# Converting v on GpSimd: one product per head with a number per partition, in place of one product of two tensors per block

## The chip, the cores and the metric

The kernel runs on one core of a Trainium2 chip. The metric is the device time of one execution in microseconds (us), lower is better. Engines: TensorE (PE; its weight loads are PEld), VectorE (DVE), ScalarE (ACT), GpSimd (POOL) and SyncE (SP, which here only issues DMAs). On-chip memory is SBUF, with 128 partitions; matmul results land in PSUM.

## What is computed

Attention with a decay by a forget gate, followed by a two-layer block with a gate (SiLU) over all tokens. Cut to what matters:

```python
batch, n_heads, seq, head_dim = (8, 8, 576, 64)
scores = scale * np.matmul(q, k.transpose(0, 1, 3, 2))
cum = np.cumsum(np.log(np.clip(f, 0.0001, 1.0)), axis=-1)
decay = cum[:, :, :, None] - cum[:, :, None, :]
scores = np.where(causal, -1000000000.0, scores + decay)
attn = softmax(scores)
x = (attn @ v) as 4608 tokens x 512
h = x @ w_in                       # 512 -> 2048
out = (h * sigmoid(h)) @ w_out     # 2048 -> 512
```

The decay factors: exp(cum_q - cum_k). The factor of the query cancels in the softmax, and the factor of the key is a weight w per key and head. The kernel therefore multiplies each row of v, and a column of ones beside it that gives the sum of the softmax, by w of that key and head.

## The kernel before

The 64 (batch, head) pairs are handled as 32 units of two heads: unit n is batch n // 4 and p = n % 4, with heads p and p + 4. The keys and queries of a sequence are cut into a first block of 128 rows, three more of 128 (`NR` = 3), and a tail of 64 (`ST`). The first blocks of all batches are done early. Then a loop over m = 0 to 15 takes two units a round; a round has a fixed order of instructions for every engine, written out by hand, in which pieces of the two matrix products of the second layer are placed between the steps of attention by a small planner (`fill`, `slot`, `rest`, `ones`). Every engine works through its own list in that order; nothing is reordered at run time.

The steps that the change and the prediction speak of:

- `load_v(b, c)` (L190): SP's queue loads rows 128 + 128c and on of v of batch b, all eight heads, as float32 into `vf`, 128 partitions x 8 heads x 65 (the last column holds ones). There are four such tiles, one for each c. The fourth block, c = 3, is the tail of 64 rows, in partitions 64 to 127.
- `convert_v(b, c)` (L429): GpSimd multiplies the block by the weights `w_bf` and writes bf16 into `vp`, of which there are two, for even and odd batches. A block of c = 0, 1, 2 is one instruction over 128 partitions x 520 elements, the weights read as a tensor repeated along the 65 columns. The tail is two instructions over 64 partitions x 260: heads 0 to 3 go to partitions 64 to 127 of the output, heads 4 to 7 to partitions 0 to 63.
- `turn(n)` is called once per unit. On GpSimd it puts, in this order: the casts of unit n + 3 to bf16 (`cast_qk`, L409 and L413, which wait for q's load), the issue of the two k transfers of unit n + 4 (`load_qk`, L160), and, in `prepare`, where p is 2 or 3, the conversion of blocks 0 and 1 (p = 2) or 2 and 3 (p = 3) of the next batch. On SP it puts the q loads of unit n + 4 (L169), v's loads of the next batch where p = 1, the tails' loads where p = 2 (L179), and then the transpose of unit n + 3 by DMA (`transposes`, L443), which waits for the casts.
- `scores(n, c)` (L475 on TensorE, L480 and L486 on ScalarE): scores of unit n and their exponentials, into `u` and, for the tail's queries, `ut`.
- `mask(n)` (L492) and `mask_tail(n)` (L498): VectorE multiplies the exponentials of the diagonal blocks by a triangle of ones, `u` x `tri` and `ut` x `trit`. Both inputs lie in SBUF.
- `attend(n)`: TensorE multiplies the exponentials by the converted v (L522; the tail's queries L531) into `dn`; VectorE takes the reciprocal of the sum (L539) and scales the result into `xr` (L540).
- `m1_chunk`: TensorE, `hp` = x times a block of w_in (L583); ScalarE, `th` = tanh of half of it (L591); VectorE, `gt` = (th + 1) x `hp` (L592), which frees `hp`. Its four PSUM buffers (tag "big") are shared with `dn`, `po` and others.
- `m2_part` (L628) and `m2_rows` (L654): `gt` times w_out, into `po` or `pr`; then a copy to SBUF and the store, issued by SP (L607).

In a round with `m2_rows`, which is nearly every one from m = 0 on, the order around the conversion is: scores of unit n, turn(n), one half of `m2_rows`, mask(n), more scores, turn(n + 1), the other half, mask_tail(n), mask(n + 1), scores, attend(n), mask_tail(n + 1), pieces of the second layer, attend(n + 1), more pieces. So p = 2 and p = 3 are the two units of an odd m, and the next batch's v is read from the following round on.

Of the kernel before, what the change touches and what calls it, by code (L numbers as in the profile page):

```python
# [9 lines left out]
ALU = mybir.AluOpType  # L10
FP32 = mybir.dt.float32
BF16 = mybir.dt.bfloat16
P = 128
# [5 lines left out]
def kernel(  # L19
# [10 lines left out]
    nc = tc.nc  # L30

    B, H, S, D = q.shape
    DM, DFF = moe_w_in.shape
    BH = B * H
    NCC = DM // P
    NFC = DFF // P
    NP = H // 2
    SM = 512
    ST = S - SM
    NM = SM // P  # L40
    NR = NM - 1
# [14 lines left out]
    const = ctx.enter_context(tc.tile_pool(name="const", bufs=1))  # L56
# [14 lines left out]
    w_in_bf = const.tile([P, NCC, DFF], BF16, name="w_in_bf")  # L71
    w_out_bf = const.tile([P, NFC, DM], BF16, name="w_out_bf")
    w_bf = const.tile([P, NM + 1, BH], BF16, name="w_bf")
    ident_bf = const.tile([P, P], BF16, name="ident_bf")
    sel = const.tile([P, 2, D], BF16, name="sel")
    ident_f = const.tile([BH, BH], FP32, name="ident_f")
# [5 lines left out]
    junk = const.tile([1, 16], BF16, name="junk")  # L82
    kT0 = [const.tile([P, NP, P], BF16, name=f"kT0_{b}") for b in range(B)]
    v0 = [const.tile([P, H, D + 1], BF16, name=f"v0_{b}") for b in range(B)]
    vps = [const.tile([P, NM, H, D + 1], BF16, name=f"vp_{i}") for i in range(2)]
    uts = [const.tile([P, NM + 1, 3, ST], BF16, name=f"ut_{i}") for i in range(4)]
    vfs = [const.tile([P, H, D + 1], FP32, name=f"vf_{i}") for i in range(4)]

# [63 lines left out]
    def head(p, i):  # L152
        return p + NP * i
# [77 lines left out]
    for i in range(2):  # L231
        nc.vector.tensor_copy(
            out=sel[:, i, :].rearrange("p (a r) -> p a r", a=NP),
            in_=ident_bf[:, :].rearrange("p (r i a) -> p i a r", i=2, a=NP)[:, i, :, :],
        )

    def keep_warm(n):
# [7 lines left out]
        out=f_sb[:, :], in0=f_sb[:, :], scalar1=1e-4, scalar2=1.0, op0=ALU.max, op1=ALU.min  # L245
# [172 lines left out]
    def convert_v(b, c):  # L418
        vbf[b] = vps[b % 2]
        if c < NR:  # L420
            parts = [(slice(0, P), slice(0, P), slice(0, H), slice(0, H))]
        else:
            parts = [
                (slice((1 - i) * ST, (2 - i) * ST), slice(ST, P), slice(0, NP), slice(i * NP, (i + 1) * NP))
                for i in range(2)
            ]
        for ro, r, ho, h in parts:
            w = w_bf[r, c + 1, b * H + h.start : b * H + h.stop, None]
            nc.gpsimd.tensor_tensor(  # L429
                out=vbf[b][ro, c, ho, :],  # L430
                in0=vst[b][c][r, h, :],
                in1=w.to_broadcast([r.stop - r.start, h.stop - h.start, D + 1]),
                op=ALU.mult,
            )
# [71 lines left out]
    def attend(n):  # L506
        b, p = divmod(n, NP)
        if p % 2 == 0:
            xqs[n // 2] = xqp.tile([P, NGR, 2, D], BF16, name="xr", tag="xr", bufs=3)
        xq = xqs[n // 2]  # L510
        u, ut = us.pop(n), uts[n % 4]
        dn = pbig.tile([P, NGR, D + 1], FP32, name="dn", tag="big")

        def vals(kb, i):
            h = head(p, i)
            return v0[b][:, h, :] if kb == 0 else vbf[b][:, kb - 1, h, :]

        for i in range(2):
            for c in range(1, NM):
                for kb in range(c + 1):  # L520
                    o = AT[c, kb]
                    nc.tensor.matmul(  # L522
                        dn[:, i * NR + c - 1, :],
                        lhsT=u[:, i, o : o + P],
                        rhs=vals(kb, i),
                        start=(kb == 0),
                        stop=(kb == c),
                    )
        for j in range(2 * NM + 1):
            kb, i = (j % NM, j // NM) if j < 2 * NM else (NM, 0)  # L530
            nc.tensor.matmul(  # L531
                dn[:, NGR - 1, :],
                lhsT=ut[:, kb, i : i + 2, :].rearrange("p i t -> p (i t)"),
                rhs=vals(kb, i) if kb < NM else vbf[b][:, NR, p, :],
                start=(j == 0),
                stop=(j == 2 * NM),
            )
        rec = recp.tile([P, NGR], FP32, name="rec", tag="rec")
        nc.vector.reciprocal(out=rec[:, :], in_=dn[:, :, D])  # L539
        nc.vector.tensor_tensor(  # L540
            out=xq[:, :, p % 2, :],
            in0=dn[:, :, 0:D],
            in1=rec[:, :, None].to_broadcast([P, NGR, D]),
            op=ALU.mult,
        )
# [280 lines left out]
    for i in range(2):  # L826
        r = slice((1 - i) * ST, (2 - i) * ST)
        nc.gpsimd.tensor_copy(out=trit[r, i, :], in_=tri[r, r])
    for t in uts:
        nc.gpsimd.memset(t[:, 0:NM, 1, :], 0.0)  # L830
    load_w_out(0)
# [62 lines left out]
    for c in range(NM):  # L894
        convert_v(0, c)
# [11 lines left out]
    def prepare(n):  # L907

        b, p = divmod(n, NP)
        if n != NP - 1 and n + 4 < NU:  # L910
            load_qk(n + 4)
        if b + 1 == B:
            return
        if p == 2 and b + 2 < B:
            load_tails(b + 2)
        if b == 0 and p >= 2 or b > 0 and p == 1:
            for c in range(NM) if b > 0 else range(2 * (p - 2), 2 * (p - 1)):
                load_v(b + 1, c)
        if n == NP - 1:
            load_qk(n + 4)  # L920
        if p >= 2:
            for c in range(2 * (p - 2), 2 * (p - 1)) if b > 0 else range(NM * (p - 2)):
                convert_v(b + 1, c)
# [56 lines left out]
    for m in range(NQ):  # L980
# [19 lines left out]
        if m > 0:  # L1000
            if m % 2 == 0:
                b = m // 2 - 1
                pending.append([1 if m == 2 else 2, [REST_OF[b]] + ([TAILS_OF[b][0]] if b == NM - 1 else [])])
        if rows:
# [12 lines left out]
            m2_out(*rows)  # L1017
            passed()
            attend(n)
            mask_tail(n + 1)  # L1020
            if late:
# [3 lines left out]
            else:  # L1025
                slot(1.9, 3)
            attend(n + 1)
            if m < 4:
                if m < 3:
# [18 lines left out]
        mask_tail(n + 1)  # L1048
        slot(piece, 0, (1, 0))
        attend(n)  # L1050
        attend(n + 1)
        slot(min(3.5, max(0.8, behind() - LAG)) if m > 1 else 0.8)
# [40 lines left out]
```

## Time and profile before

| | us |
|---|---|
| median of 3 runs | 339.35 |
| lowest, highest | 338.65, 339.97 |
| the profiled execution, its own time | 341.14 |
| its span, first to last instruction | 339.4 |

Mean granted TensorE clock of the profiled execution: 0.999 of full speed.

| engine | busy us | share of the span | instructions |
|---|---|---|---|
| TensorE | 326.7 | 96% | 4268 |
| TensorE's weight loads | 229.2 | 68% | 4292 |
| ScalarE | 217.2 | 64% | 385 |
| VectorE | 200.5 | 59% | 435 |
| GpSimd | 139.5 | 41% | 223 |

The profile is of one execution; times count from the first instruction. In its lists of groups a row reads: line, engine, operation, output<-inputs with their shapes, count | busy us, mean ns of one | idle us of the engine before them, and what ended that. In a timeline a row reads: start, duration, engine, line, operation, output<-inputs, count of merged instructions, and in brackets how long the engine was idle before and what released it. Neighbours of one kind are merged into one row. An instruction's duration can overlap the next one's start a little.

### The profile page before, as it was taken

Reading aid. Unit: us, or ns where it says so; the run is one execution under the profiler, and the core shown is the slowest. Engines: PE = TensorE matmul, PEld = TensorE weight load, DVE = VectorE, ACT = ScalarE, POOL = GpSimd, SP = SyncE. Lnnn points to the kernel's source line nnn. Section 1 sums busy time; section 2 is a strip of 40 time slices with the busy share of each in tenths; the row PEclk is TensorE's granted clock in tenths of the full one; section 3 lists DMA queues with packets and bytes.
Section 4 is the critical chain, followed back from the end, with each engine's and each line's share of the span. In section 5 each row is a group of like instructions: output and inputs, shape, how many; then the busy total and the mean of one; then the engine's idle time right before and its main releaser. Section 6 shows DMA issues by size and latency. Waiting matters only on the chain.

```text
span 339.4 us, 10334 instructions
## 1 busy us (share of the span) xinstructions
PE 326.7 (96%) x4268; PEld 229.2 (68%) x4292; DVE 200.5 (59%) x435; ACT 217.2 (64%) x385; POOL 139.5 (41%) x223
## 2 busy tenths in 40 slices
PE   7999999999999999999999997999999999999995
PEld 3745566798786767758857894867676676555654
DVE  4668745369568467565656965886673557344330
ACT  5767546687777577758748792866776486344431
POOL 8894426574764664464474352628060000000000
PEclk9999999999999999999999999999999999999999
DMA  8999999999999998997999789959973110001012
GB/s 155 187 189 220 180 215 164 241 171 172 182 188 170 168 186 158 194 190 150 181 179 165 147 148 147 156 115 188 151 108 87 53 38 33 34 33 59 34 62 63
DMA packets 144703, 48.01 MB, mean 141 GB/s; under 512 B 133328, under 2 KB 139728, under 8 KB 144656
## 3 DMA queue, kind: packets, MB, share of 16 engines
q1 hardware_dynamic: 115088, 36.60, 56.9%
q0 software_dynamic: 29408, 10.62, 27.0%
q8 instruction: 33, 0.54, 0.7%
q10 hardware_dynamic: 160, 0.13, 0.2%
q14 instruction: 14, 0.11, 0.1%
HBM read 36.85 MB, written 9.44 MB: 136 GB/s over the span
## 4 chain that ended last, share of the span: by engine, by line
PE 85%; DMA 6%; DVE 4%; POOL 2%; issue 1%; ACT 1%; SPq 1%; POOLq 0%
PE hp L583 33%; PE po L628 20%; PE pr L654 15%; PE sc L475 6%; PE dn L522 5%; DMA vf<-in_v_dram 3%; PE dn L531 2%; DMA qkb<-in_k_dram 1%; PE tp L293 1%; DVE gt L592 1%; DMA qf<-in_q_dram 1%; DVE ut L498 1%; DVE u L343 1%; SPq L443 1%; POOL vp L429 1%
## 5 line engine op out<-in xcount | busy, mean ns | idle before, releaser
L591 ACT ACTIVATE th<-hp 128x384 bf16<-128x384 f32 (+2 forms) x208 | 96.5, 468 | 75.0 <-PE hp L583 68.8
L592 DVE SCALAR_TENSOR_TENSOR gt<-th,hp 128x384 bf16<-128x384 bf16 (+2 forms) x208 | 107.5, 523 | 54.3 <-ACT th L591 44.3
L583 PE MATMUL hp<-x,w_in_bf 128*128 128x384 bf16 (+2 forms) x701 | 120.6, 321 | 0.7 <-DVE gt L592 0.4
L583 PEld LDWEIGHTS <-w_in_bf 128*128 128x128 bf16 x832 | 79.0, 98 | 50.2 <-issue 3.7
L486 ACT ACTIVATE u<-sc 128x1024 bf16<-128x1024 f32 (+1 forms) x96 | 74.3, 811 | 6.9 <-PE sc L475 6.9
L628 PE MATMUL po<-w_out_bf,gt 128*128 128x512 bf16 (+1 forms) x316 | 74.1, 368 | 1.4 <-DVE gt L592 0.2
L654 PE MATMUL pr<-w_out_bf,gt 64*128 64x256 bf16 x1024 | 61.4, 269 | 0.0
L409 POOL CAST qkb<-qf 128x384 bf16<-128x384 f32 x32 | 17.3, 542 | 88.9 <-DMA qf<-in_q_dram 88.3
L654 PEld LDWEIGHTS <-gt 64*128 64x128 bf16 x1024 | 51.2, 94 | 3.9
L628 PEld LDWEIGHTS <-gt 128*128 128x128 bf16 x336 | 32.2, 98 | 27.4 <-issue 0.3
L160 POOL DMA_DIRECT2D qkb<-in_k_dram x56 | 43.9, 786 | 0.8 <-issue 0.7
L429 POOL TENSOR_TENSOR vp<-vf,w_bf 128x520 bf16<-128x520 f32 (+1 forms) x40 | 36.5, 915 | 14.0 <-DMA vf<-in_v_dram 11.9
L638 ACT ACTIVATE osb<-po 128x512 f32<-128x512 f32 (+1 forms) x21 | 12.1, 577 | 26.5 <-PE po L628 26.5
L475 PE MATMUL sc<-qkT 64*128 64x128 bf16 (+1 forms) x640 | 28.2, 206 | 0.4 <-DMA qkT<-qkb 0.3
L492 DVE TENSOR_TENSOR u<-u,tri 128x768 bf16<-128x768 bf16 x32 | 20.2, 631 | 13.5 <-ACT u L486 13.5
L475 PEld LDWEIGHTS <-qkT 64*128 64x128 bf16 x640 | 20.3, 94 | 7.6 <-issue 4.7
L480 ACT ACTIVATE ut<-sc 128x640 bf16<-128x640 f32 x32 | 22.4, 701 | 3.0 <-PE sc L475 2.5
L522 PEld LDWEIGHTS <-u 128*128 128x128 bf16 x576 | 20.6, 97 | 3.1
L522 PE MATMUL dn<-vp,u 128*128 128x65 bf16 x384 | 21.8, 193 | 0.0
L540 DVE TENSOR_TENSOR xr<-dn,rec 128x448 bf16<-128x448 f32 x32 | 20.0, 625 | 1.1
L522 PE MATMUL dn<-v,u 128*128 128x65 bf16 x192 | 20.0, 194 | 0.0
L665 DVE COPY fence<-pr 128x1 f32<-128x1 f32 x16 | 2.5, 158 | 28.0 <-PE pr L654 28.0
(70 smaller groups left out, 243.4 us busy)
## 6 DMA issues: line engine op xcount, KB each, us to landing
out_dram<-osb SPq DMA_DIRECT2D x32, 256.0 KB, 2.9
vf<-in_v_dram SPq DMA_DIRECT2D x26, 256.0 KB, 5.1
qf<-in_q_dram SPq DMA_DIRECT2D x64, 96.0 KB, 3.3
qkb<-in_k_dram POOLq DMA_DIRECT2D x56, 48.0 KB, 4.0
w_in_bf<-in_moe_w_in_dram POOLq DMA_DIRECT2D x4, 512.0 KB, 6.8
w_out_bf<-in_moe_w_out_dram POOLq DMA_DIRECT2D x4, 512.0 KB, 9.1
vf<-in_v_dram POOLq DMA_DIRECT2D x6, 256.0 KB, 9.6
qkb<-in_q_dram POOLq DMA_DIRECT2D x8, 128.0 KB, 4.9
```

Of the source, the lines that this page charges most:

```text
L160: nc.gpsimd.dma_start(out=t2[:, NR + 1 : NX, j * D : (j + 1) * D], in_=k[b, head(p, j), P:SM, :].rearrange("(c p) d -> p c d", p=P),)
L429: nc.gpsimd.tensor_tensor(out=vbf[b][ro, c, ho, :], in0=vst[b][c][r, h, :], in1=w.to_broadcast([r.stop - r.start, h.stop - h.start, D + 1] ...
L475: nc.tensor.matmul(sc[:, i, o : o + q1 - q0], lhsT=kt, rhs=t[r, q0:q1], start=True, stop=True)
L480: nc.scalar.activation(out=ut[:, :, 0:3:2, :].rearrange("p k i t -> p i k t"), in_=sc[:, :, T0 : T0 + (NM + 1) * ST].rearrange("p i (k t) ...
L486: nc.scalar.activation(out=u[:, :, c * SM : c * SM + w], in_=sc[:, :, 0:w], func=ACT.Exp, scale=scale)
L492: nc.vector.tensor_tensor(out=x, in0=x, in1=tri[:, None, None, :].to_broadcast([P, 2, NR, P]), op=ALU.mult)
L522: nc.tensor.matmul(dn[:, i * NR + c - 1, :], lhsT=u[:, i, o : o + P], rhs=vals(kb, i), start=(kb == 0), stop=(kb == c),)
L583: nc.tensor.matmul(hp[:, :], lhsT=w_in_bf[:, cc, fc * P : (fc + 1) * P], rhs=xcols(g, cc), start=(cc == 0), stop=(cc == NCC - 1),)
L591: nc.scalar.activation(out=th[:, :], in_=hp[:, :], func=ACT.Tanh, scale=0.5)
L592: nc.vector.scalar_tensor_tensor(out=gt[:, fc, :], in0=th[:, :], scalar=1.0, in1=hp[:, :], op0=ALU.add, op1=ALU.mult,)
L628: nc.tensor.matmul(po[:, :], lhsT=gt[:, fc, tb * P : (tb + 1) * P], rhs=w_out_bf[:, fc, m0:m1], start=(fc == 0), stop=(fc == NFC - 1),)
L654: nc.tensor.matmul(pos[g, tb][y], lhsT=gt[r, fc, tb * P : (tb + 1) * P], rhs=w_out_bf[r, fc, y * DM // 2 : (y + 1) * DM // 2], start=(half ...
```

## The change

A float32 copy `w_f` of the weights is made once on GpSimd, ahead of the loop. For batches two to seven, `convert_v` issues one `tensor_scalar` for each head: 128 partitions x 65 elements (64 x 65 in the tail), multiplied by one number per partition, which is read from `w_f`. Blocks 0 to 2 take eight instructions each and the tail two times four, so that a batch takes 32 in place of 5. Batches 0 and 1 keep the product of two tensors. The tile `vp` is laid out anew: 3 x 8 + 4 head columns in one dimension in place of 4 blocks x 8 heads, and the readers' index follows.

```diff
+    w_f = const.tile([P, NM, BH], FP32, name="w_f")
...
-    vps = [const.tile([P, NM, H, D + 1], BF16, name=f"vp_{i}") for i in range(2)]
+    vps = [const.tile([P, NR * H + NP, D + 1], BF16, name=f"vp_{i}") for i in range(2)]
...
         for ro, r, ho, h in parts:
+            if b > 1:
+                for x in range(h.stop - h.start):
+                    z = b * H + h.start + x
+                    nc.gpsimd.tensor_scalar(
+                        out=vbf[b][ro, c * H + ho.start + x, :],
+                        in0=vst[b][c][r, h.start + x, :],
+                        scalar1=w_f[r, c, z : z + 1],
+                        scalar2=None,
+                        op0=ALU.mult,
+                    )
+                continue
             w = w_bf[r, c + 1, b * H + h.start : b * H + h.stop, None]
             nc.gpsimd.tensor_tensor(
-                out=vbf[b][ro, c, ho, :],
+                out=vbf[b][ro, c * H : c * H + ho.stop, :],
                 in0=vst[b][c][r, h, :],
                 in1=w.to_broadcast([r.stop - r.start, h.stop - h.start, D + 1]),
                 op=ALU.mult,
...
-            return v0[b][:, h, :] if kb == 0 else vbf[b][:, kb - 1, h, :]
+            return v0[b][:, h, :] if kb == 0 else vbf[b][:, (kb - 1) * H + h, :]
...
-                rhs=vals(kb, i) if kb < NM else vbf[b][:, NR, p, :],
+                rhs=vals(kb, i) if kb < NM else vbf[b][:, NR * H + p, :],
...
+    nc.gpsimd.tensor_copy(out=w_f[:, :, :], in_=w_bf[:, 1 : NM + 1, :])
     for t in uts:
         nc.gpsimd.memset(t[:, 0:NM, 1, :], 0.0)
```

## The prediction

> **What bounds the kernel now.** I read the page's busy slices first, then the stretches, then TensorE's, VectorE's and GpSimd's timelines where TensorE has a hole. The slices of TensorE and GpSimd (each digit is a fortieth of the span, 8.5 us):
>
> ```profile
> PE   7999999999999999999999997999999999999995
> POOL 8894426574764664464474352628060000000000
> ```
>
> TensorE is full from the second slice to the last but one, apart from one 7, the slice from 203.6 us. GpSimd has time to spare and ends at 252 us. The stretches give each engine's busy time in 30 us (PE, PEld, DVE, ACT, POOL):
>
> ```profile
> 170.00:200.00 30.00, 29.93 (x400) 22.32 (x402) 20.57 (x46) 21.88 (x43) 14.19 (x22) 1.00 0.93 158
> 200.00:230.00 30.00, 27.71 (x391) 20.28 (x388) 21.62 (x40) 19.63 (x36) 12.48 (x20) 1.00 0.91 145
> 230.00:260.00 30.00, 29.89 (x416) 21.01 (x414) 19.21 (x38) 19.21 (x34) 12.53 (x19) 1.00 0.87 136
> ```
>
> Converting batches two to seven lies between 99 and 251 us. In that time TensorE stands still for 2.3 us near 203, and for under 0.5 us elsewhere. So the most that this change can win is about 2.7 us, 0.8%. TensorE's hole, and what VectorE did at that moment:
>
> ```profile
> 202.00 1.91 PE L583 MATMUL hp<-xt,w_in_bf 128*128 128x256 bf16 x16
> 206.15 0.60 PE L583 MATMUL hp<-xt,w_in_bf 128*128 128x256 bf16 x4 [2.24 <-DVE gt L592]
> ```
>
> ```profile
> 202.99 2.78 DVE L498 TENSOR_TENSOR ut<-ut,trit 128x128 bf16<-128x128 bf16 x1
> 205.69 1.93 DVE L592 SCALAR_TENSOR_TENSOR gt<-th,hp 128x256 bf16<-128x256 bf16 x5
> ```
>
> `mask_tail` (L498) takes 0.226 us in the median of its 32 and here took 2.78. The gate products (L592) queue behind it on VectorE, they empty the `hp` buffers, and TensorE waits 2.24 us for a buffer. GpSimd at that time:
>
> ```profile
> 201.33 0.50 POOL L409 CAST qkb<-qf 128x384 bf16<-128x384 f32 x1 [0.48 <-DMA qf<-in_q_dram]
> 201.78 0.29 POOL L413 CAST qkb<-qktf 128x128 bf16<-128x128 f32 x1
> 202.02 1.56 POOL L160 DMA_DIRECT2D qkb<-in_k_dram  x2
> 203.60 2.08 POOL L429 TENSOR_TENSOR vp<-vf,w_bf 128x520 bf16<-128x520 f32 x2
> ```
>
> The mask ends 0.1 us after the two v products (203.60 + 2.08 = 205.68). The same pair meets at 234.88: the mask takes 2.44 and ends at 237.32, the products at 237.23. There TensorE had `po` products that need nothing of VectorE, so nothing was lost. All told the two masks, which have both inputs in SBUF, are some 9.7 us over their usual lengths (0.55 and 0.22) in the run; the gate products and `xr`, with one input in PSUM, keep theirs. So a mask and a reading GpSimd instruction hold each other up. This holds for other reading instructions too:
>
> ```profile
> 232.63 0.84 DVE L492 TENSOR_TENSOR u<-u,tri 128x768 bf16<-128x768 bf16 x1 [0.96 <-ACT u L486]
> 232.56 0.50 POOL L409 CAST qkb<-qf 128x384 bf16<-128x384 f32 x1 [0.41 <-DMA qf<-in_q_dram]
> 233.01 0.61 POOL L413 CAST qkb<-qktf 128x128 bf16<-128x128 f32 x1
> ```
>
> The mask waits 0.3 us, goes in between the two casts, and the second cast (usually 0.29) waits in turn. The mask waited for one short instruction, not for both.
>
> **The change part by part.** *The price of one new instruction, t.* The trace has no product with a number per partition. The rows next to it:
>
> ```profile
> L429 POOL TENSOR_TENSOR vp<-vf,w_bf 128x520 bf16<-128x520 f32 x24 | 25.3, 1061 | 12.9 <-DMA vf<-in_v_dram 11.9 <-PE hp L583 0.7
> L429 POOL TENSOR_TENSOR vp<-vf,w_bf 64x260 bf16<-64x260 f32 x16 | 11.1, 697 | 1.1
> L828 POOL COPY trit<-tri 64x64 bf16<-64x64 bf16 x2 | 0.5, 234 | 0.1
> ```
>
> From below: the 384-element cast starts 0.45 before the next instruction and the 128-element one 0.24 (starts above), so 0.82 ns an element and 0.135 fixed; 65 elements make 0.19. From above: a product of 260 elements, 0.62 at its shortest. I take 0.24, the copy of 64 elements, nearest in size, and keep 0.19 and 0.62 for the range.
>
> *GpSimd's work.* A full block goes from one product, about 1.02 from start to start, to eight instructions, 8 x 0.24 = 1.92. The last block goes from two of 0.70 to eight, 1.92. A batch goes from 3 x 1.02 + 2 x 0.70 = 4.5 to 32 x 0.24 = 7.7, six batches add 19 us. They come in trains: blocks 0 and 1 in the turn of a batch's third unit (2.08 becomes 3.84), blocks 2 and 3 in the fourth's (2.44 to 2.80 becomes 3.84).
>
> *What stands behind the trains.* No new wait is added; the first instruction of a block waits for its v transfer as before. Behind a train on GpSimd's queue stand the next unit's two casts and its two k transfers; behind the casts, on SP, that unit's transpose, and behind that stores and the next q loads. After a train of blocks 0 and 1 GpSimd sits idle for 4.9 to 9.3 us for q (before the casts at 107.59, 131.67, 157.07, 182.64, 214.97, 245.91), which swallows 1.8. After blocks 2 and 3 the next cast follows at once in five of six places and would be 1.0 to 1.4 us late. Its units are 11, 15, 19 and so on; counting 24 score products to a unit, unit 11's transpose is issued at 115.09 and its first score stands at 127.00, the others have 14 us or more, a transpose lands in 3.8: nothing lost.
>
> *Who reads the v blocks.* Batches 3 to 7 are read 5 us or more after their last product (136.4 against 141.5, later 6.7 and 13). Batch 2 is tight:
>
> ```profile
> 109.88 2.66 POOL L429 TENSOR_TENSOR vp<-vf,w_bf 128x520 bf16<-128x520 f32 x3
> 114.66 0.28 PE L531 MATMUL dn<-vp,ut 128*128 128x65 bf16 x4
> ```
>
> The last tail product, about 114.7, needs heads 0 and 4 of block 3, the thirteenth instruction of the train: 109.88 + 13 x 0.24 = 113.0, plus the two masks that go in between (0.55 and 0.22): 113.8. Nothing at 0.24; TensorE begins to wait at t = (114.7 - 109.88 - 0.77) / 13 = 0.31 us, and then loses 13 x (t - 0.31). I book 0.1 for this.
>
> *The copy of the weights*, once, 256 elements: by the cast's line 0.35, near 22.8 us. GpSimd idles 4.42 for v at 29.75, but two w_out issues (23.81) go 0.35 later, and SP's later loads wait for one of them (until 35.67). The DMA engines are nine tenths busy there and have older transfers queued: between 0 and 0.35, I book 0.1. The smaller v tile and its new index move no time.
>
> *The masks.* Between instructions of 0.24 the mask waits as it did between the casts, 0.3 at most. At 203 the 2.24 us go; next late there would be TensorE's own order, since `gt` would follow its `th` as in the other rounds. The excess elsewhere cost TensorE nothing and wins nothing.
>
> The Trainium skill, SBUF — State Buffer, Who interferes with whom, speaks against more than that: a VectorE instruction with two SBUF inputs and a GpSimd instruction that reads SBUF exclude each other for a whole instruction. The new one still reads SBUF, so by that page the conflict is cut small and not removed; the trace agrees at 232.63 (0.3 us for one cast), and by it the sum is the same.
>
> **Sum.** 341.14 (own time; span 339.4 and 1.7 around it) - 2.24 + 0.1 + 0.1 = 339.1. The median shown, 339.35, is 1.8 below the profiled execution. I assume that the hole at 203 is in the timed runs too, as the order is fixed, and take the difference as the price of profiling: 339.35 - 2.04 = **337.3**.
>
> **Rivals.**
> - *No change that shows.* The collision needs the mask to arrive within some 2.5 us of a train whose start hangs on a q transfer's landing (0.48 of waiting at 201.33). The 1.8 us between the profiled and the timed runs are near the 2.24: if the timed runs miss the collision, nothing can be won, 339.35 + 0.2 = 339.5. The same if t is 0.40: batch 2 gives back 13 x 0.09 = 1.2, and 338.4 remains. About 339.
> - *The instruction is dear (slower).* At t = 0.62 TensorE waits 13 x 0.31 = 4.0 us for batch 2 at 114.7: 339.35 + 4.0 - 2.2 = 341.1, or 343.5 if the stall at 203 isn't in the timed runs; it decides from t = 0.31 and makes the kernel slower by over 0.5% from 0.61, or 0.44 without the stall. For it: nothing shows what fetching the number costs. Against it: all one-input rows of this size are at 0.3 or below.
> - *The train stays closed (slower).* At 203 the mask didn't get in between the two products (the first ended near 204.67), but behind the second. If sixteen short ones in a row leave no opening either, it waits until 203.60 + 3.84 = 207.44 in place of 205.68, and TensorE 1.8 longer; at 234.88 the same makes up to 1.7 more: 341.1 to 342.8, say 342. Against it: at 217.37 the mask got in after 1.07 us, with a train of three of 2.80. The Trainium skill, GPSIMD Engine Reference, Instruction dispatch, says that the eight cores don't hold each other at the end of an instruction; cores out of step would leave no common gap. The trace agrees at 203 (both products were sat out) and not at 217.
> - That the change doesn't do what it says: the counts would tell (192 instructions in place of 30); I give it nothing.
>
> **Chances.** Forecast 0.42 (336.3 to 337.6: the lower end wins all 2.7 and some of the edges), no change 0.30, dear 0.15, closed train 0.13. What a measurement of this kernel can tell from no change is about 0.5%, 1.7 us: faster than 337.65, 0.42; slower than 341.05, 0.28; between, 0.30. The range reaches from 336.3 to 341.4: it leaves out the worse half of the two slower cases and a little below. The forecast's own range is 336.3 to 338.
>
> **What would show it.** Right: no L498 over 0.8 us, no hole over 0.5 us near 203, new GpSimd instructions at 0.19 to 0.30 from start to start, first `dn` of batch 2 unmoved. Dear: t over 0.31 and a TensorE wait on `vp` near 114. Closed: an L498 of 3 us or more beside a train. The forecast is wrong if the timed runs never had the hole, or if later starts of trains make new collisions where TensorE has only gate work.

## The result and the profile after

| | before | after |
|---|---|---|
| median, us | 339.66 (6 runs, the first three among them) | 343.33 (6 runs) |
| lowest, highest | 338.65, 341.44 | 341.23, 346.23 |
| the profiled execution, own time (span) | 341.14 (339.4) | 345.39 (343.6) |

The ratio is 1.012, 95% interval 1.0087 to 1.0154: the change made the kernel slower by 3.7 us. The page of the changed kernel, slices of the span (lines of the kernel file move by 1 to 13; `mask_tail` is now L510, `mask` L504, the new instruction L432, the old products L441):

```profile
PE   8999999999799799999999999999999999999995
POOL 8985416554779959898798797969679100000000
PEclk9999999999999989999999999999999999999999
```

TensorE's 7 near 203 us is gone. There are others in the slices from 86 and from 112 us, and just behind the second the granted clock dips. GpSimd is busy until 267 us. The stretches (busy us of PE, PEld, DVE, ACT and POOL, then the granted clock, the DMA share and GB/s):

```profile
90.00:130.00 40.00, 37.34 (x531) 26.45 (x529) 24.61 (x56) 25.03 (x44) 31.42 (x63) 0.96 1.13 155
...
170.00:200.00 30.00, 29.47 (x430) 21.94 (x430) 18.35 (x42) 21.16 (x37) 25.75 (x52) 1.00 1.16 159
200.00:230.00 30.00, 30.00 (x447) 23.29 (x445) 19.21 (x48) 21.98 (x42) 23.41 (x49) 1.00 0.96 151
230.00:260.00 30.00, 30.00 (x430) 21.77 (x429) 18.99 (x43) 21.65 (x38) 23.56 (x48) 1.00 1.16 156
```

From 200 us on TensorE has no hole at all. The loss lies before, above all between 90 and 130. TensorE's timeline at its largest hole, and GpSimd's in front of it:

```profile
116.02 0.25 PE L543 MATMUL dn<-vp,ut 128*128 128x65 bf16 x3
118.46 0.19 PE L543 MATMUL dn<-vp,ut 128*128 128x65 bf16 x1 [2.19 <-POOL vp L432]
```

```profile
101.81 6.94 POOL L432 TENSOR_SCALAR vp<-vf,w_f 128x65 bf16<-128x65 f32 x16 [1.20 <-DMA vf<-in_v_dram]
109.41 0.51 POOL L410 CAST qkb<-qf 128x384 bf16<-128x384 f32 x1 [0.66 <-DMA qf<-in_q_dram]
...
111.75 8.28 POOL L432 TENSOR_SCALAR vp<-vf,w_f 128x65 bf16<-128x65 f32 x16
120.10 0.51 POOL L410 CAST qkb<-qf 128x384 bf16<-128x384 f32 x1
```

The train of batch 2's blocks 2 and 3 takes 8.28 us, where the old one took 2.66. The tail product of batch 2's first unit waits 2.19 us for its thirteenth instruction. The list of waits for TensorE from 95 to 200 us (total, times, longest) has this and two smaller ones, at 148 us (0.59, batch 3) and 176 us (0.51, batch 4):

```profile
PE dn L543 <- POOL vp L432: 3.3, 3, 2.2
```

What the hole brought with it shows in narrow stretches (columns as above):

```profile
116.20:119.60 3.40, 1.21 (x10) 0.55 (x7) 0.88 (x3) 0.91 (x3) 2.84 (x8) 0.99 0.42 88
119.60:123.00 3.40, 3.40 (x17) 1.48 (x16) 0.09 (x1) 0.00 (x0) 3.33 (x7) 0.50 0.32 45
```

In 3.4 us TensorE was busy for 1.21, and for the next 3.4 us it was granted half its clock. The 3.4 us of work done there would have taken 1.7 at the full clock, so this costs 1.7 us more.

**Where the 4.2 us of the two profiled executions come from.** I line up the first score product of each unit in both (before, after):

| up to unit | before | after | later by | step |
|---|---|---|---|---|
| 4 | 83.43 | 83.46 | 0.03 | |
| 6 | 96.01 | 97.36 | 1.35 | +1.3, at 87 and 91 us, batch 1, not converted in the new way |
| 10 | 124.42 | 129.79 | 5.37 | +4.0, batch 2: wait 2.19, half clock 1.7 |
| 14 | 152.54 | 158.67 | 6.13 | +0.8, batch 3 |
| 18 | 182.00 | 188.79 | 6.79 | +0.7, batch 4 |
| 22 | 213.56 | 217.97 | 4.40 | -2.4, no hole near 203 |
| 31 | 277.09 | 281.39 | 4.29 | -0.1 |

The three waits on v add up to 3.3 us, near the 3.7 between the medians; only one of the six timed executions was profiled, so how the others divide is not shown. The other steps vary from execution to execution. The 1.3 near 90 us were 0.4 in the kernel of e1 below and 1.4 in that of e5, whose programs are alike up to there. The two runs of the changed kernel that show a granted clock of 1.000 took 342.74 and 342.86 us, against 345.39 for the profiled one (0.995); the fastest, 341.23, shows 0.998.

### The profile page after: what moved, and what is told of

Same layout as the page of the kernel before. It is cut to its first block, busy times and chain, and to the rows that moved or that the text cites. A ratio compares the mean times of both kernels' runs of the same rounds, so it can differ in the third digit from the quotient of the medians.

```text
span 343.6 us, 10508 instructions
## 1 busy us (share of the span) xinstructions
PE 332.0 (97%) x4292; PEld 230.3 (67%) x4292; DVE 194.3 (57%) x435; ACT 217.3 (63%) x385; POOL 200.3 (58%) x386
## 4 chain that ended last, share of the span: by engine, by line
PE 66%; DMA 13%; POOL 12%; SPq 3%; DVE 2%; issue 2%; ACT 1%; POOLq 0%
PE hp L595 24%; PE po L640 19%; PE pr L666 10%; DMA qf<-in_q_dram 6%; POOL vp L432 5%; PE sc L487 4%; DMA vf<-in_v_dram 4%; PE dn L534 4%; DMA w_out_bf<-in_moe_w_out_dram 3%; PE dn L543 2%; SPq L455 2%; POOL v L349 1%; PE wm L241 1%; POOL qkb L161 1%; PE tp L294 1%
## 5 line engine op out<-in xcount | busy, mean ns | idle before, releaser
L432 POOL TENSOR_SCALAR vp<-vf,w_f 128x65 bf16<-128x65 f32 (+1 forms) x192 | 88.6, 478 | 5.6 <-DMA vf<-in_v_dram 1.2
L640 PE MATMUL po<-w_out_bf,gt 128*128 128x512 bf16 (+1 forms) x336 | 79.1, 374 | 0.2
L504 DVE TENSOR_TENSOR u<-u,tri 128x768 bf16<-128x768 bf16 x32 | 19.0, 593 | 15.0 <-ACT u L498 15.0
L551 DVE RECIPROCAL rec<-dn 128x7 f32<-128x7 f32 x32 | 6.5, 204 | 22.4 <-PE dn L543 22.4
```

What stands on the lines that cost most here:

```text
L432: nc.gpsimd.tensor_scalar(out=vbf[b][ro, c * H + ho.start + x, :], in0=vst[b][c][r, h.start + x, :], scalar1=w_f[r, c, z : z + 1], scalar2 ...
L640: nc.tensor.matmul(po[:, :], lhsT=gt[:, fc, tb * P : (tb + 1) * P], rhs=w_out_bf[:, fc, m0:m1], start=(fc == 0), stop=(fc == NFC - 1),)
```

## The experiments

My theory after this result ("late v", later "price"): the new instruction costs about 0.43 us, nearly twice what I took, and the loss is batch 2 reaching its reader late, with batches 3 and 4 behind it; the collision with the masks is solved. Rivals: the loss comes from the copy of the weights at the start ("start"); or longer trains cost something in every batch ("load"). All diffs are against the changed kernel.

**e1, the copy and the layout alone.**

```diff
-            if b > 1:
+            if b > B:
```

> The copy of the weights and the new layout of vp stay; all batches are converted by products of two tensors again. Theory 'late v' (the new instruction takes 0.44 us, so batches 2 to 4 are read before they are ready, which costs 2.2, 0.6 and 0.5 us and a spell at half clock; the collision near 203 is gone, which wins 2.2): same time as before, within 0.5 us, and the long mask_tail with its hole of some 2 us is back in odd rounds from 200 us on. Rival 'start' (the 1.3 us that the profiled execution of the changed kernel lost between 84 and 92 us, where batch 1 is read, come from the copy and what it delays): 1 to 1.5 us slower than before.

Ratio to before 1.0003, interval 0.9978 to 1.0027. The rival "start" falls. But the expected hole near 203 wasn't there in the profiled execution, though the products were the old ones: one `mask_tail` took 2.46 us, at 233, and TensorE lost nothing by it. That pointed at the hole itself (e11).

**e2, batches 5 to 7 alone.**

```diff
-            if b > 1:
+            if b > 4:
```

> Per-head instructions for batches 5, 6 and 7 alone. Theory 'late v': these batches had 13 us between their last product and their first reader, trains of 7 to 8 us fit, no wait of TensorE on vp from 100 us on, and the collisions at 203 and 235 are gone: 1 to 2.3 us faster than before (337.4 to 338.7). Rival 'load' (longer trains delay the casts, the k transfers and SP's queue in every batch): half of the loss stays, 341 or more. If the timed runs of before don't have the hole: same as before.

338.89 against 339.26, ratio 0.9974, interval 0.9948 to 0.9999. No wait of TensorE on `vp` past 100 us, so half of the new instructions cost nothing, and "load" falls. The gain, 0.4 us between the medians and 0.9 by the ratio, is below the least expected, and the interval all but reaches 1.

**e3, batches 2 to 4 alone.**

```diff
-            if b > 1:
+            if 1 < b <= 4:
```

> Per-head instructions for batches 2, 3 and 4 alone. Theory 'late v': the waits on vp at about 116, 148 and 176 us stay and the hole near 203 may come back: 2 to 5 us slower than before, at least as slow as the changed kernel. Rival 'load': about half of the loss, 1.5 to 2 us slower than before.

342.36, ratio 1.0098, interval 1.0063 to 1.0133: 3.1 us above before, nearly the whole loss. TensorE's waits in the profile (1.64 at 114 us, 1.64 at 144, 0.50 at 173):

```profile
PE dn L543 <- POOL vp L432: 3.8, 3, 1.6
```

**e4, blocks 0 and 1 of batches 5 to 7.**

```diff
-            if b > 1:
+            if b > 4 and c < 2:
```

> Per-head instructions only for blocks 0 and 1 of batches 5 to 7, the trains that met mask_tail near 203 and 235. Theory 'late v': as the version for whole batches 5 to 7, 1 to 2.3 us faster than before, since the trains of blocks 2 and 3 (near 217 and 249) cost TensorE nothing before. Rival 'load': between that version and before.

338.85, ratio 0.9985, interval 0.996 to 1.001: not told apart from before, where 1 to 2.3 us less was expected.

**e5, e6, e7: the price of one instruction.** In place of the number per partition: the constant 1.0 (e5); a plain copy (e6); a product of two tensors per head (e7). e5 and e6 leave out the weights of batches 2 to 7.

```diff
-                        scalar1=w_f[r, c, z : z + 1],
+                        scalar1=1.0,
```

```diff
-                    nc.gpsimd.tensor_scalar(
+                    nc.gpsimd.tensor_copy(
                         out=vbf[b][ro, c * H + ho.start + x, :],
-                        in0=vst[b][c][r, h.start + x, :],
-                        scalar1=w_f[r, c, z : z + 1],
...
+                        in_=vst[b][c][r, h.start + x, :],
                     )
```

```diff
-                    nc.gpsimd.tensor_scalar(
+                    nc.gpsimd.tensor_tensor(
...
-                        scalar1=w_f[r, c, z : z + 1],
-                        scalar2=None,
-                        op0=ALU.mult,
+                        in1=w_bf[r, c + 1, z : z + 1].to_broadcast([r.stop - r.start, D + 1]),
+                        op=ALU.mult,
                     )
```

> The same instructions with the constant 1.0 in place of the number per partition; leaves out the weights of batches 2 to 7. If fetching the number makes the price: 0.19 to 0.25 us from start to start in place of 0.44. If a scalar instruction of this size costs that whatever the number: 0.4 or more.

> A plain copy with conversion for each head, 65 elements; leaves out the weights of batches 2 to 7. By the casts' line 0.19 us, by the 64-element copy 0.24, from start to start. If cutting into 32 instructions were itself dear: 0.4 or more.

> A product of two tensors for each head, 65 elements. By the line through the 520-element and 260-element products (1.02 and 0.70) it would take 0.46, as dear as the new instruction; if the 260-element ones are dear because they wait for each other, 0.25. Masks: if any short reading instruction lets a mask in, no mask over 0.3 us late.

GpSimd's groups (busy us, mean ns of one) of the changed kernel, and of e5, e6 and e7 in this order:

```profile
L432 POOL TENSOR_SCALAR vp<-vf,w_f 128x65 bf16<-128x65 f32 x144 | 65.4, 476 | 1.6 <-DMA vf<-in_v_dram 1.2
L432 POOL TENSOR_SCALAR vp<-vf,w_f 64x65 bf16<-64x65 f32 x48 | 23.2, 483 | 3.9
```

```profile
L432 POOL TENSOR_SCALAR vp<-vf 128x65 bf16<-128x65 f32 x144 | 50.7, 387 | 1.5 <-DMA vf<-in_v_dram 1.1
```

```profile
L432 POOL CAST vp<-vf 128x65 bf16<-128x65 f32 x144 | 27.8, 242 | 0.2 <-DMA vf<-in_v_dram 0.2
```

```profile
L432 POOL TENSOR_TENSOR vp<-vf,w_bf 128x65 bf16<-128x65 f32 x144 | 38.1, 298 | 0.3
```

An instruction's duration can overlap the next one's start, so I compare medians from start to start (one profiled execution of each), and set beside them how long TensorE waited for batch 2:

| per head, full block | start to start, us | TensorE's wait near 115 us |
|---|---|---|
| copy (e6) | 0.179 | none |
| product of two tensors (e7) | 0.252 | none |
| constant number (e5) | 0.335 | 1.20 |
| number per partition (changed kernel) | 0.422 | 2.19 |

The wait follows the price: thirteen instructions, 13 x (0.422 - 0.335) = 1.13 us more, and the wait grows by 0.99. The constant's 0.335 lies between the two values that I expected. Fetching the number is 0.09 of the price; most of it is the kind of instruction. A product with a second tensor, repeated along the row, is cheaper than a multiplication by one number. In the tail the new instructions stand 0.53 apart: there each begins some 0.08 us after the one before has ended, while in a full block it begins 0.02 before that. Why is not shown; the per-head products stand 0.25 apart in the tail too.

**e8, products of four heads.**

```diff
-                for x in range(h.stop - h.start):
+                n4 = min(4, h.stop - h.start)
+                for x in range(0, h.stop - h.start, n4):
                     z = b * H + h.start + x
-                    nc.gpsimd.tensor_scalar(
-                        out=vbf[b][ro, c * H + ho.start + x, :],
...
+                    nc.gpsimd.tensor_tensor(
+                        out=vbf[b][ro, c * H + ho.start + x : c * H + ho.start + x + n4, :],
...
```

> Blocks 0 to 2 of batches 2 to 7 as two products of four heads, 260 elements, in place of one of eight. Theory 'late v': trains grow by under 1 us, batch 2's last block comes near 113.5, so no wait of TensorE on vp over 0.3 us; what is left is whether a mask gets in between such products: if yes the time is 1 to 2 us below before, if the train stays closed to it, as at 203, equal to before.

339.54 against 339.44, ratio 0.9995, interval 0.9972 to 1.0017. No wait on `vp` past 100 us. The masks next to trains are up to 0.76 us late (984 ns in place of 225), and none of it reaches TensorE. So a mask got in and the time stayed equal, which neither branch of the expectation had.

**e9, a product per head, timed** (the kernel of e7).

> The product of two tensors for each head of batches 2 to 7, as in the single look before (0.25 us from start to start, no wait on vp), now timed. Theory 'price' (what costs is the price of one instruction against batch 2's deadline, not the cutting): not slower than before; 338.2 to 339.3. Rival 'cutting' (32 instructions a batch cost in themselves): 340 or more.

338.85 against 338.90, ratio 0.9997, interval 0.9979 to 1.0016. Cutting a batch's conversion into 32 instructions costs nothing; the kind of instruction does. And it wins nothing either, although these instructions have almost the price, 0.25, that the prediction took.

**e10, batches 3 to 7.**

```diff
-            if b > 1:
+            if b > 2:
```

> The changed kernel with batch 2 converted by products again; batches 3 to 7 per head with a number per partition. Theory 'price': batch 2's wait near 115 us goes, and with it any half-clock spell behind it; batch 3 and 4 may still make TensorE wait, 0.5 to 1.6 us each: 339.5 to 341.5, at least 1.5 us below the changed kernel. If the loss is spread evenly over six batches: 342.5.

339.16 against 338.90, ratio 1.002, interval 0.9994 to 1.0046. This is 0.3 us below the range that I expected. Leaving one batch of six to the old products takes back nearly all: the loss hangs on batch 2. In this kernel TensorE waits nowhere from 95 to 200 us. GpSimd's train of blocks 2 and 3 of batch 2, and the tail product of batch 2's first unit:

```profile
110.95 2.66 POOL L441 TENSOR_TENSOR vp<-vf,w_bf 128x520 bf16<-128x520 f32 x3
```

```profile
115.66 0.28 PE L543 MATMUL dn<-vp,ut 128*128 128x65 bf16 x4
```

Batches 3 and 4 no longer make TensorE wait, so their 0.59 and 0.51 in the changed kernel, and batch 3's 1.64 in e3, needed batch 2's long trains ahead of them.

**e11, the kernel before, once more.** No edit.

> The kernel before, unchanged, profiled once more. If the hole of 2.2 us near 203 us belongs to the fixed order: it is there again. If it belongs to single executions: no hole, and a time near 339.

338.42 us, span 336.6, and no hole. VectorE and GpSimd at the place where the first profile had the mask of 2.78 us:

```profile
202.24 0.62 DVE L540 TENSOR_TENSOR xr<-dn,rec 128x448 bf16<-128x448 f32 x1
202.78 0.22 DVE L498 TENSOR_TENSOR ut<-ut,trit 128x128 bf16<-128x128 bf16 x1
203.07 1.95 DVE L592 SCALAR_TENSOR_TENSOR gt<-th,hp 128x256 bf16<-128x256 bf16 x5
```

```profile
201.68 1.56 POOL L160 DMA_DIRECT2D qkb<-in_k_dram  x2
203.26 2.25 POOL L429 TENSOR_TENSOR vp<-vf,w_bf 128x520 bf16<-128x520 f32 x2
```

Here the mask started 0.48 us ahead of the two products and took its usual 0.22. In the first profile it started 0.61 ahead, even earlier, and was caught. In both it started while GpSimd was issuing k's transfers, and 0.22 us would have ended before the first product. So these starts don't tell the two cases apart, and what held the mask from 202.99 to 203.60 is not shown. Of five profiled executions in which products of two tensors convert batch 5 there (before, e1, e3, e8, e11) one has the hole. Without it there was nothing to win: from the first score product of unit 18 to that of unit 31 TensorE takes 92.6 us in e11, in e2 and in the changed kernel alike, against 95.1 in the first profile.

**e12, one instruction for a whole block, with a constant.** Leaves out the weights of batches 2 to 7.

```diff
-                for x in range(h.stop - h.start):
...
+                nc.gpsimd.tensor_scalar(
+                    out=vbf[b][ro, c * H : c * H + ho.stop, :],
+                    in0=vst[b][c][r, h, :],
+                    scalar1=1.0,
...
```

> One instruction of 520 elements (260 in the tail's halves) with the constant 1.0 in place of eight; leaves out the weights of batches 2 to 7. Against 0.34 us for 65 elements it parts the fixed price from the price of an element: if the fixed part is 0.28, some 0.7 to 0.8 us for 520 elements.

```profile
L430 POOL TENSOR_SCALAR vp<-vf 128x520 bf16<-128x520 f32 x18 | 27.4, 1529 | 2.1 <-DMA vf<-in_v_dram 1.3 <-PE hp L593 0.4
```

1.488 us from start to start, twice what was expected: the price lies in the elements. (1.488 - 0.335) / 455 = 2.5 ns an element and 0.17 fixed, against (1.017 - 0.252) / 455 = 1.7 ns for the product of two tensors.

## Why the prediction failed

- **The step that failed: "I take 0.24, the copy of 64 elements, nearest in size".** The term is the price t; it measured 0.42 in full blocks and 0.53 in the tail. I chose the row by size and not by kind of operation. I worked out 0.8 ns an element from the casts and carried this over to a multiplication by a number; e12 shows three times as much. The trace of before has no row of the right kind on GpSimd: a product of two tensors per head, had it been shown, would have given 0.25 (e7). Only the upper end of the range, 0.62, allowed for what came.
- **Batch 2's deadline: right place, right mechanism.** The thirteenth instruction of that train, the threshold, and nothing at 0.24 are what e7 shows (0.25: no wait). The threshold of 0.31 was too high: at 0.335 it gives 13 x 0.025 = 0.3 us of wait, and e5 had 1.20. In the changed kernel the train began at 111.75, with TensorE 1.35 behind, so 0.5 later against TensorE than before; and the tail's instructions cost 0.11 more than the others, five of them 0.6. The rival "the instruction is dear" gives 13 x (0.42 - 0.31) = 1.4 at the measured price, that is 340.8 to 341 without the gain at 203, so it had the cause and the sign, but less than half of the loss. I had given it 0.15.
- **"I assume that the hole at 203 is in the timed runs too, as the order is fixed": wrong.** e11, e1 and e3 don't have it. The order is fixed, but the start of a train follows a q transfer, and the profile of one execution can't tell a hole of the program from a hole of that execution. The 1.8 us between the profiled execution and the median was largely the hole, not the price of profiling: e11 was profiled at 338.42. So the gain of 2.24 that the forecast rested on was not there in four of five profiled executions. In e9, at 0.25 an instruction, almost the price that I took, the time is the same as before: without the hole the forecast of a gain fails at that price too, and the dear instruction turned nothing into a loss.
- **The masks: right.** Beside the new trains no mask was more than 0.2 us late, and GpSimd gave way (an instruction of 0.44 took up to 0.86). VectorE's masks during a train of the changed kernel (158.51 to 165.76):

```profile
161.15 0.65 DVE L504 TENSOR_TENSOR u<-u,tri 128x768 bf16<-128x768 bf16 x1
...
163.20 0.56 DVE L504 TENSOR_TENSOR u<-u,tri 128x768 bf16<-128x768 bf16 x1 [0.96 <-ACT u L498]
```

  The rival "the train stays closed" falls with this.
- **What stands behind the trains: half right.** The trains were longer than I took them (up to 8.3 us in place of 3.8), so the casts behind them moved by more, and GpSimd's idle time after a train of blocks 0 and 1 shrank to between 0.7 and 3.6 us. It held from batch 5 on; batches 3 and 4 lost 1.1 us together, and lose nothing where batch 2's trains are short (e10).
- **The copy of the weights: right**, nothing (e1).
- **The half clock was not in the working.** In the profiled execution it cost 1.7 us behind the 2.19.

## What to carry to other kernels

Price a new instruction by a row of its own kind of operation; a row of the same size but another kind is a guess. For the same 65 elements a copy stood 0.18 us apart here, a product of two tensors 0.25 and a multiplication by a number per partition 0.42. Where the profile has no such row, let the range and the chances follow the dearest neighbour; here a threshold of 0.31 lay between two rows and decided the sign. A hole seen in one execution, where two engines happened to meet, is not yet a cost of the program: look for it in a second execution before counting on its removal. When a stage is slack on average, find the one consumer with a deadline; five of six batches took the dearer conversion at no cost that shows (e10). Of the seven other versions timed, the one with batches 5 to 7 alone (e2) is the only one whose interval lies below before, by 0.3%; with an upper end of 0.9999 and no gain in its trace, that isn't shown to be more than chance.

## What the runs showed of the hardware

- On GpSimd a multiplication by one number (float32 in, bf16 out) is dearer per element than a product of two tensors: 2.5 against 1.7 ns, a cast 0.8. A number per partition in place of a constant adds 0.09 us an instruction. The Trainium skill, GPSIMD Engine Reference, Engine selection, calls operations of one input roughly line rate and those of two inputs about twice as slow as VectorE's. Here the cast is indeed the cheapest, but the multiplication by one number costs more than the product of two tensors, and the measurement decides.
- TensorE's granted clock fell to 0.50 for 3.4 us after a hole of 2.19 us; the hole of 2.24 us in the profile of before had no such spell behind it. The Trainium skill, TensorE: Matmul & The Clock Gate, Part 1, tells of windows of about 3.4 us that run on freely, and of a clock set by how busy TensorE was. The length of the spell agrees. TensorE had worked 1.21 of the 3.4 us just before the spell. It also worked only 1.16 between 203.00 and 206.40 in the profile of before, with no spell behind it, so the amount of work in 3.4 us doesn't decide alone; where the windows fell no run here shows.
- Beside two products of 1.02 us back to back on GpSimd a mask, with two SBUF inputs, was up to 2.6 us late (at 203 in the first profile; 2.2 at 235 there and at 233 in e1) and ended about when the second product did. In e11 the mask in the same place took its usual time. Beside trains of short instructions (0.25 or 0.42 us) no mask was more than 0.2 us late in the changed kernel, e7 and e9. Why the boundary between the two long ones gave no opening was not settled.
